# Products of zeros in row tiles of 128, 64 and 32 rows behind the warm-up of an attention and gated-MLP kernel

## The chip, the cores and the metric

The kernel runs on one core of a Trainium2 chip. The metric is the device time of one execution in microseconds (us); lower is better. The core's engines work side by side, each through its own instructions in order: PE (TensorE, matrix products; its loads of weights are listed as PEld), DVE (VectorE), ACT (ScalarE), POOL (GpSimd) and SP (SyncE, which here only issues DMAs). The time before is the median of two runs, 1200.67 us (1200.6 and 1200.75).

## The reference

The inputs are x (2048 tokens of 448 features), wqkv (448 x 1344), wo (448 x 448), W_gate and W_up (448 x 1792), W_down (1792 x 448) and a vector gate_w (448), all float32. An attention block with 16 heads of 28 and a gated MLP are both computed on x and mixed, token by token, by a sigmoid:

```python
x = A_x
g = sigmoid((x * gate_w).sum(-1, keepdims=True))
qkv = (x @ wqkv)                      # split into q, k, v, 16 heads of 28
p = softmax(q @ k.T * 28 ** -0.5)
a = (p @ v) @ wo
gate = x @ W_gate
b = ((gate * (gate > 0)) * (x @ W_up)) @ W_down
return g * a + (1 - g) * b
```

## The kernel before

PE multiplies at its fast rate in the format float32r. To keep float32's accuracy, x, the weights and q and k are split into a high part (the value rounded to float32r, written by ACT in `act_high`, L121) and a low part (the rest, a subtraction on DVE in `low`, L127), and a product of two such numbers is a sum of several products; the table TERMS (L74) lists eleven of them for the 448-deep sums, two chunks of rows being packed together where 64 rows are left over.

The order of all engines' work is written out by hand (`manual_schedule`): an engine executes its instructions in the order in which the kernel's code issues them, and semaphores only make an instruction wait for its operands.

The stages on PE are:

1. A warm-up of WARM = 11 products of a bfloat16 tile of zeros, `warm`, into one PSUM tile (L469 to L472). They need nothing but a memset on DVE, and run while the first loads of x and wq are under way.
2. The projection (`qk`, L427, and `vproj`, L445): for each of four blocks of 512 tokens, seven columns of q and k and the v columns, eleven products each, in PSUM tiles of 512 columns. Each q and k result is copied out by ACT and DVE and sent to DRAM by POOL's queue (L435), and read back by SP's queue as K (L167) and Q (L175). Its last part is mixed with the products that find the scores' maxima (`smax`, L200).
3. The attention, 32 rounds: scores (`score`, L306), their maxima, exponentials on ACT, and P times V (`pv`, L653). In P·V, four products of 32 columns of V each write their own 32 partitions of one PSUM tile; V and P are plain float32 there. The gate and up products of the MLP (L600) fill gaps.
4. The output projection (L852) and the down projection (L893).

The steps around the change, in the order of the code: the loads of the first weights and of x (`load_w`, L341; `load_x`, L377; `load_first`, L459), the warm-up, `make_identity` on POOL, memsets on POOL of rows 96 to 127 of two K tiles and two Q tiles (L479, L480: `f32(K[k])[96:128]` and `f32(QS[k])[96:128]`, k = 0, 1) and of parts of V (L482, L483), the split of the first weights and the first block of x (`split_first`), the split of the second weight chunk (`split_w`), then the first real product group, `qk(0, 0, BY_CHUNK)`, then `split_x(1, x1)`, `load_x(2)` and so on. QS holds the Q tiles, `[128, 4, 512]` in float32r; the second, QS[1], is first filled with a head's q late in the projection.

PSUM has eight banks of 512 float32 columns for each partition. Tiles with the tag "mx" are pairs of banks, of which there are two; they first serve the scores' maxima in the second half of the projection. The warm-up and the first product groups use banks with other tags ("x" and "s").

Of the kernel before, what the change touches and what calls it, by code (L numbers as in the profile page):

```python
# [8 lines left out]
F32 = mybir.dt.float32  # L9
# [9 lines left out]
P = 128  # L19
# [9 lines left out]
TB = 512  # L29
# [55 lines left out]
def gated_mix_kernel(ctx, tc, x, wq, wo, wgu, wd, out):  # L85
    nc = tc.nc
# [3 lines left out]
    psum = ctx.enter_context(tc.tile_pool(name="psum", bufs=1, space=PSUM))  # L90
# [3 lines left out]
    def f32(ap):  # L94
        return ap.bitcast(F32)
# [53 lines left out]
    QS = [vp.tile([P, 4, TB], F32R, name=f"Q{r}") for r in range(2)]  # L149
# [184 lines left out]
    with tc.tile_pool(name="qkv", bufs=1) as pa:  # L334
# [133 lines left out]
        warm = pa.tile([P, TB], BF16, name="warm")  # L468
        nc.vector.memset(warm, 0.0)  # L469
        ps = ps_x("warm_ps")  # L470
        for n in range(WARM):
            nc.tensor.matmul(ps, warm[:, :P], warm, start=True, stop=True)  # L472

        ident = const.tile([P, P], F32, name="ident")
        make_identity(nc, ident)
# [264 lines left out]
    for v, order in enumerate(ROUNDS):  # L740
# [4 lines left out]
        for o in order:  # L745
# [12 lines left out]
            elif o == "x":  # L758
                i, half, n = passes.pop(0)
# [228 lines left out]
```

## Time and profile before

| | |
|---|---|
| median of the runs | 1200.67 us |
| profiled execution: its span, first to last instruction | 1198.9 us |
| granted clock of PE, mean | 1.000 |
| PE products (L600, gate and up) | 1232, busy 364.6 us |
| PE products (L306, scores) | 1024, busy 316.8 us |
| PE products (L653, P·V) | 2048, busy 363.6 us in two groups |
| PE products (L427, q and k) | 308, busy 77.4 us |
| idle time of PE before its first product | 1.2 us, ended by the memset of `warm` |

Every line of a timeline of the profile gives the start in us from the first instruction, the length, the engine, the line of the kernel, the operation, what it writes and reads, "rows*columns" of the weights for PE, the shape of the other operand, how many instructions are merged in the line, and in brackets the idle time of the engine before them and what ended it. The durations of PE's products are modelled ends of a pipeline, so the distance from one start to the next tells more than the length of one. A line of the chain gives start, length and the work that the end of the program hung on at that time. A line of the windows view gives a stretch, its length, the busy time and number of instructions of PE, PEld, DVE, ACT and POOL, PE's granted clock, and the share and rate of the DMA engines.

### The profile page before, as it was taken

How to read it: one execution, taken by the hardware profiler on the slowest of the kernel's cores; microseconds unless marked ns; L12 is line 12 of the kernel's file. 1: busy time of each engine (PE TensorE's matmuls, PEld its weight loads, DVE VectorE, ACT ScalarE, POOL GpSimd, SP SyncE). 2: the span in 40 equal slices, each digit the busy share in tenths (PEclk: the TensorE clock that was granted, in tenths of full speed). 3: DMA queues.
4: the chain of work that ended last, by engine and by line, in shares of the span. 5: the costliest groups of instructions: out<-in, count | busy, mean ns of one | idle time of the engine just before them, and what ended most of it. 6: DMA issues, size and time to landing. Idle time of an engine off the chain costs nothing.

```text
span 1198.9 us, 16948 instructions
## 1 busy us (share of the span) xinstructions
PE 1183.7 (99%) x6183; PEld 820.1 (68%) x6183; DVE 902.8 (75%) x1179; ACT 878.2 (73%) x1082; POOL 748.9 (62%) x326
## 2 busy tenths in 40 slices
PE   9999999999999999999999999999999999999998
PEld 6888755556656666666666666666666666899997
DVE  6466798888898989898888989898988653544242
ACT  5321789999999888888788888888888896422121
POOL 4222387889897777766676767777767786522020
PEclk9999999999999999999999999999999999999999
DMA  9956354354535453443536443436443425743342
GB/s 317 319 207 250 136 191 137 111 141 143 156 129 159 148 163 114 124 122 117 150 119 186 118 129 110 128 117 191 112 126 105 138 89 161 218 136 119 114 128 75
DMA packets 63486, 178.35 MB, mean 149 GB/s; under 512 B 13050, under 2 KB 19650, under 8 KB 58754
## 3 DMA queue, kind: packets, MB, share of 16 engines
q1 hardware_dynamic: 56812, 151.53, 41.1%
q0 software_dynamic: 6160, 25.30, 5.5%
q8 instruction: 48, 0.79, 0.3%
q10 hardware_dynamic: 432, 0.46, 0.1%
q14 instruction: 34, 0.28, 0.1%
HBM read 118.58 MB, written 58.87 MB: 148 GB/s over the span
## 4 chain that ended last, share of the span: by engine, by line
PE 85%; DVE 5%; ACT 3%; DMA 3%; issue 1%; POOL 1%; SPq 1%; DVEq 0%; POOLq 0%; ACTq 0%
PE gu L600 19%; PE s L306 18%; PE po L653 18%; PE sm L200 10%; PE acc L893 10%; PE qk L427 6%; PE wo L852 3%; PE v L445 3%; DVE r L256 1%; ACT P L310 1%; DVE mx L204 1%; ACT P L312 1%; ACT P L296 1%; DMA ls<-os 1%; DMA wor<-wo_d 1%
## 5 line engine op out<-in xcount | busy, mean ns | idle before, releaser
L285 POOL TENSOR_TENSOR P<-P,rm 128x2048 f32<-128x2048 f32 x102 | 470.7, 4633 | 95.5 <-DVE rm L279 79.7
L600 PE MATMUL gu<-X,wg 128*128 128x512 f32 x1232 | 364.6, 395 | 0.7 <-ACT rl L610 0.7
L204 DVE TENSOR_REDUCE mx<-sm 128x1 f32<-128x1024 f32 x256 | 301.5, 1215 | 40.9 <-PE sm L200 40.5
L306 PE MATMUL s<-Q,K 128*128 128x512 f32 x1024 | 316.8, 405 | 6.2 <-ACT V L310 1.9
L600 PEld LDWEIGHTS gu<-X,wg 128*128 128x128 f32 x1232 | 231.2, 188 | 56.7 <-ACT rl L610 2.0
L306 PEld LDWEIGHTS s<-Q,K 128*128 128x128 f32 x1024 | 178.1, 188 | 98.5 <-DVE mn L265 13.4
L312 ACT ACTIVATE P<-s 128x1024 f32<-128x1024 f32 x204 | 202.9, 1031 | 44.2 <-PE s L306 41.6
L653 PE MATMUL po<-P,V 128*32 128x512 f32 x1640 | 227.7, 594 | 0.4 <-ACT P L296 0.4
L296 ACT ACTIVATE P<-P 128x1024 f32<-128x1024 f32 x204 | 213.2, 1072 | 2.1 <-POOL P L285 1.8
L310 ACT ACTIVATE P<-s 128x1024 f32<-128x1024 f32 x206 | 201.5, 1039 | 9.0 <-PE s L306 7.7
L256 DVE SCALAR_TENSOR_TENSOR r<-s,r 128x1024 f32<-128x1024 f32 x124 | 151.6, 1223 | 19.0 <-ACT P L312 10.5
L200 PE MATMUL sm<-K,Q 128*128 128x512 f32 x520 | 163.7, 399 | 0.7 <-DVE mx L204 0.6
L653 PEld LDWEIGHTS po<-P,V 128*32 128x32 f32 x1640 | 63.5, 110 | 116.3 <-issue 108.8
L653 PE MATMUL po<-V 128*32 128x512 f32 x408 | 135.9, 594 | 0.0
L285 POOL TENSOR_TENSOR V<-V,rm 128x2048 f32<-128x2048 f32 x24 | 111.1, 4634 | 23.0 <-DVE rm L279 19.3
L121 ACT ACTIVATE hh<-hr 128x512 fp32r<-128x512 f32 x52 | 32.8, 631 | 117.9 <-PE acc L893 111.8
L200 PEld LDWEIGHTS sm<-K,Q 128*128 128x128 f32 x520 | 91.3, 188 | 33.2 <-ACT P L310 5.6
L127 DVE TENSOR_TENSOR hh<-hr,hh 128x512 fp32r<-128x512 f32 x52 | 47.8, 926 | 82.6 <-ACT hh L121 78.9
L893 PE MATMUL acc<-WD,hh 128*128 128x448 f32 x480 | 100.7, 368 | 0.0
L893 PEld LDWEIGHTS acc<-WD,hh 128*128 128x128 f32 x480 | 90.1, 188 | 8.8
L256 DVE SCALAR_TENSOR_TENSOR r<-s,P 128x1024 f32<-128x1024 f32 x50 | 61.1, 1223 | 38.3 <-ACT P L312 38.3
L271 DVE TRANSPOSE_TENSOR_REDUCE mn<-r 128x32 f32<-128x1024 f32 x63 | 78.0, 1238 | 1.3
(87 smaller groups left out, 1142.6 us busy)
## 6 DMA issues: line engine op xcount, KB each, us to landing
wg<-ws_d SPq DMA_DIRECT2D x42, 896.0 KB
K<-qk_d SPq DMA_DIRECT2D x32, 448.0 KB
Q<-qk_d SPq DMA_DIRECT2D x64, 224.0 KB
h_d<-h SPq DMA_DIRECT2D x56, 256.0 KB
hr<-h_d SPq DMA_DIRECT2D x52, 256.0 KB
ws_d<-wg SPq DMA_DIRECT2D x14, 896.0 KB
qk_d<-st POOLq DMA_DIRECT2D x21, 512.0 KB, 3.2
wgr<-wgu SPq DMA_DIRECT2D x13, 512.0 KB
```

The lines of the kernel that those rows point to most:

```text
L200: nc.tensor.matmul(ps[:, c, :], Q[h][:, u * P:(u + 1) * P], K[h % 3][:, k0:k0 + TB], start=True, stop=True)
L204: nc.vector.tensor_reduce(to, ps, axis=AX.XY, op=OP.max)
L256: nc.vector.scalar_tensor_tensor(r, ps, -1.0, before, op0=OP.mult, op1=OP.min)
L271: nc.vector.tensor_reduce(MN[:, 1:3], R2.pop((v, j)).rearrange("p a (b r) -> p a b r", r=32), axis=AX.X, op=OP.min, apply_transpose=True)
L285: nc.gpsimd.tensor_tensor(QUAD[q], QUAD[q], m, op=OP.subtract)
L296: nc.scalar.activation(q, q, AF.Exp, scale=-SCALE)
L306: nc.tensor.matmul(ps[:, c], K[h % 3][:, k * P:(k + 1) * P], Q[h][:, j * TB:(j + 1) * TB], start=True, stop=True)
L310: nc.scalar.activation(dst, ps, AF.Exp, scale=SCALE)
L312: nc.scalar.activation(dst, ps, AF.Copy, scale=-1.0)
L600: nc.tensor.matmul(ps, WS[i][:, s, a], xf(i // NF, b), start=(n == 0), stop=(n == NT - 1))
L653: nc.tensor.matmul(po[32 * j:32 * j + 32], V[:, h // 4 % 2, k, h % 4], AT.pop((v, k, j)), start=(k == k0), stop=(k == k0 + NK // 2 - 1))
L893: nc.tensor.matmul(ACC[i // NF][t][:, :D], HH[i][:, a, t * P:(t + 1) * P], wd_high_low(f, b), start=(f == 0 and n == 0), stop=(f == NF - 1 ...
```

## The change

Behind the eleven products of the warm-up, 121 more products are issued on PE. For 115 of them both operands are `z`, 512 columns of the second Q tile in float32r, set to zero by one more memset on DVE; they write four banks of the two "mx" tiles, and nobody reads the results. A "place" is one full product of 128 rows, or the two products of 64 rows or four of 32 rows that share those rows: each of them takes its rows of z and has a bank of its own. The list of (rows, count, columns of the weights) has 63 places. Six more products of the bfloat16 zeros follow. Since z lies in QS[1], the memset on POOL at L480 for k = 1, which stands behind it in the code and writes rows 96 to 127 of it, comes after the products on z.

```diff
         for n in range(WARM):
             nc.tensor.matmul(ps, warm[:, :P], warm, start=True, stop=True)
+
+        z = QS[1][:, 0]
+        nc.vector.memset(f32(z), 0.0)
+        four = [psum.tile([P, 2, TB], F32, tag="mx", bufs=2, name=f"four_{k}") for k in range(2)]
+        four = [t[:, k] for t in four for k in range(2)]
+
+        def tiles(rows, count, columns=P):
+            for n in range(count):
+                for k in range(P // rows):
+                    r = slice(k * rows, (k + 1) * rows)
+                    nc.tensor.matmul(four[k if rows < P else n % 4][:columns], z[r, :columns], z[r], start=True, stop=True)
+
+        for rows, count, columns in ((128, 10, 128), (64, 10, 128), (32, 10, 128), (128, 3, 128), (32, 3, 128), (128, 2, 128),
+                                     (32, 1, 128), (128, 2, 128), (128, 10, 64), (128, 10, 32), (128, 2, 128)):
+            tiles(rows, count, columns)
+        for n in range(6):
+            nc.tensor.matmul(four[n % 4], warm[:, :P], warm, start=True, stop=True)
 
         ident = const.tile([P, P], F32, name="ident")
```

## The prediction

> **What bounds the kernel now.** I read the page first (busy shares, then the chain that ended last), then the chain of the first 30 us in order of time, then the PE and PEld timelines around the warm-up. The page:
>
> ```profile
> span 1198.9 us, 16948 instructions
> PE 1183.7 (99%) x6183; PEld 820.1 (68%) x6183; DVE 902.8 (75%) x1179; ACT 878.2 (73%) x1082; POOL 748.9 (62%) x326
> PE 85%; DVE 5%; ACT 3%; DMA 3%; issue 1%; POOL 1%; SPq 1%; DVEq 0%; POOLq 0%; ACTq 0%
> ```
>
> PE is busy 99% of the span and carries 85% of the chain, so work put on PE ahead of everything else is paid unless PE stood idle there. The chain of the first 30 us, with a later row of it for the pace, and PE busy by stage (PE busy and count first in each windows row):
>
> ```profile
> 3.12 5.80 DMA wr<-wq
> ...
> 8.95 0.49 ACT W L121
> ...
> 9.46 0.94 DVE W L127 x2
> 10.40 0.04 issue
> 10.45 19.67 PE qk L427 x84
> ...
> 50.22 2.53 PE qk L427 x11
> ```
>
> ```profile
> 10.40:38.40 28.00, 27.95 (x121) 22.78 (x122) 18.45 (x27) 14.81 (x25) 7.84 (x12) 1.00 0.92 321
> 38.40:120.00 81.60, 81.60 (x374) 69.70 (x373) 48.04 (x51) 18.20 (x47) 17.91 (x27) 1.00 0.68 255
> ```
>
> Until 10.45 us a load of the weights wq and its splitting carry the chain; from 10.45 on the projection's products do, one after another, and PE has no hole up to 120 us. A dense product of 512 columns costs 2.53 / 11 = 0.230 us. What PE does before that:
>
> ```profile
> 0.87 0.27 DVE L469 MEMSET warm<- 128x256 uint32 x1 [0.87 <-PEq L981]
> 1.20 4.10 PE L472 MATMUL warm_ps<-warm 128*128 128x512 bf16 x11 [1.20 <-DVE warm L469]
> 3.74 0.15 PEld L472 LDWEIGHTS <-warm 128*128 128x128 bf16 x1 [0.28 <-issue]
> 4.16 0.15 PEld L472 LDWEIGHTS <-warm 128*128 128x128 bf16 x1 [0.27 <-issue]
> 4.82 0.39 DVE L127 TENSOR_TENSOR W<-wr,W 128x224 fp32r<-128x224 f32 x1 [3.68 <-ACT W L121]
> 5.36 3.53 PE L427 MATMUL qk<-X,W 128*128 128x512 f32 x10
> 9.06 0.49 PE L427 MATMUL qk<-X,W 128*128 128x512 f32 x1 [0.16 <-DVE X L127]
> 9.86 28.57 PE L427 MATMUL qk<-X,W 128*128 128x512 f32 x121 [0.31 <-ACT W L121]
> ```
>
> ```profile
> 4.70 0.38 PE L472 MATMUL warm_ps<-warm 128*128 128x512 bf16 x1
> ...
> 4.92 0.38 PE L472 MATMUL warm_ps<-warm 128*128 128x512 bf16 x1
> ```
>
> The warm-up starts at 0.42 us from product to product (3.74, 4.16) and ends at 0.22 (4.70, 4.92): PE is at its fast pace before the new code begins, and free at 4.92 + 0.22 = 5.14. The first real product starts at 5.36, so PE's hole there is 0.2 us. From then to 10.45 it runs only 10 + 1 + 1 = 12 products, each as its split arrives.
>
> **The change, part by part.**
>
> *Memset of z* (DVE, 128x512 f32): twice the elements of the 0.27 us memset of warm, directly behind it, so about 0.5 us and done by 1.7. DVE's next work starts at 4.82, and PE reaches z at 5.14. Cost 0, hidden by the warm-up; were that cover gone, at most 0.5 us.
>
> *The 63 places.* The list gives 10+10+10+3+3+2+1+2+10+10+2 = 63 places: 19 of full products, 10 of two products of 64 rows, 14 of four products of 32 rows, 20 with 64 or 32 columns of weights. In products these are 19 + 20 + 56 + 20 = 115, all streaming 512 columns in the format of the real products. No row of the trace has fewer than 128 rows. The nearest are those of the P·V products, four column tiles of 32 side by side:
>
> ```profile
> 180.07 7.00 PE po L653 x64
> ```
>
> ```profile
> 180.45 0.13 PEld L653 LDWEIGHTS po<-P,V 128*32 128x32 f32 x4 [0.30 <-issue]
> 180.88 0.13 PEld L653 LDWEIGHTS po<-P,V 128*32 128x32 f32 x4 [0.30 <-issue]
> ```
>
> Four weight loads start together and the next four 0.43 us later, and 64 products take 7.00 us, 0.44 per four: tiles do run at once here. In the code these P and V tiles are plain F32, whereas z, like the operands of the 0.230 us products, is F32R; so I read the 0.43 as the price of the type, not of the tiles. I take a place at one dense product, 0.230 us: 63 x 0.230 = 14.5 us. Ends: 0.22 per place (13.9), and every product for itself, 115 x 0.230 = 26.5.
>
> In a sentence apart: the Trainium skill, TensorE: Matmul & The Clock Gate, Part 3 (Measured speedup vs the span model), gives four row tiles of 32 rows a speed-up of 3.07 rather than 4; by that a place of 32 rows would cost 4 / 3.07 x 0.230 = 0.30, 14 places 1.0 us more, and the sum would be 1216.7; no run here shows it yet.
>
> *Going from one tile size to another.* The sequence has ten such places, seven of rows, three of columns. The P·V stage shows the price:
>
> ```profile
> 179.67 0.40 PE L200 MATMUL sm<-K,Q 128*128 128x512 f32 x1
> 180.00 1.07 PE L653 MATMUL po<-P,V 128*32 128x512 f32 x8
> ...
> 186.47 0.60 PE L653 MATMUL po<-P,V 128*32 128x512 f32 x2
> 187.00 0.73 PE L306 MATMUL s<-Q,K 128*128 128x512 f32 x2
> 187.57 0.62 PE L200 MATMUL sm<-K,Q 128*128 128x512 f32 x2
> ```
>
> Into the narrow tiles: 0.33 from start to start where 0.23 is the pace, 0.10 more. Out of them: 0.53 where 0.43 is the pace, and the first two products take 0.73, not 0.62, as the second weight load was not hidden: together 0.21. The row tiles load 128 columns of weights, so I take 0.2 for each of the seven, 0.1 each for going to 64 and to 32 columns, and 0.2 back: 1.8 us. Ends: 0, and 10 x 0.3 = 3.0.
>
> *Six more warm-up products*: 6 x 0.22 = 1.3 us.
>
> New work on PE: 14.5 + 1.8 + 1.3 = 17.6 us, from 5.14 to 22.7.
>
> *What the delay gives back.* Before, 12 products took 10.45 - 5.14 = 5.31 us because each waited for a split. At 22.7 all of these splits have long been made (the last, of W for the second column block, ends at 9.46 + 1.42 = 10.9, row below), so they take 12 x 0.230 = 2.76. Back: 2.55 us. The last of these waits is what is late in before; behind it nothing is late until X of the second token block:
>
> ```profile
> 9.46 1.42 DVE L127 TENSOR_TENSOR W<-wr,W 128x336 fp32r<-128x336 f32 x4 [0.46 <-ACT W L121]
> 10.08 0.58 ACT L121 ACTIVATE st<-qk 128x512 fp32r<-128x512 f32 x1
> 10.56 2.00 ACT L121 ACTIVATE X<-xr 128x1024 fp32r<-128x1024 f32 x2
> 10.91 0.69 DVE L127 TENSOR_TENSOR st<-qk,st 128x512 fp32r<-128x512 f32 x1
> 11.64 2.36 DVE L127 TENSOR_TENSOR X<-xr,X 128x1024 fp32r<-128x1024 f32 x2
> ...
> 18.20 1.06 ACT L121 ACTIVATE X<-xr 128x1024 fp32r<-128x1024 f32 x1 [3.59 <-DMA xr<-x]
> ```
>
> ACT and DVE take work in order, so this split stands behind the copy of the first product group, which moves with PE. That group ended at 9.06 + 0.49 = 9.55, and the low half of X was whole at 11.64 + 2.36 = 14.0, 4.45 us later (some 4.0 if ACT is free at once, as it is in after). The group that needs it starts one group, 2.53 us, after that end, and reads the second half of the low part from its tenth product, at 2.53 + 9 x 0.23 = 4.6: room of 0.15 to 0.6 us. SP's loads of x and wq wait for the same releases or are already there; POOL's and SP's later issues move along. Cost 0, at most 0.5.
>
> *POOL.* z lies in the second Q tile, so the memset of its rows 96 to 127 now waits for the last product on z:
>
> ```profile
> 6.61 1.81 POOL L480 MEMSET Q<- 32x2048 f32 x1
> 8.48 0.32 POOL L482 MEMSET V<- 128x256 f32 x1
> ...
> 10.30 0.21 POOL L483 MEMSET V<- 128x64 f32 x1
> ...
> 11.91 0.80 POOL L435 DMA_DIRECT2D qk_d<-st  x1 [1.41 <-DVE st L127]
> ```
>
> Behind it on POOL stand eight memsets of V and the first send of q and k. From 22.7 - 1.3 = 21.4 POOL needs 1.81 + (10.51 - 8.48) = 3.8 us, to 25.2; the data of the first send are there at 25.2 + 2.05 (as 11.60 against 9.55 before), 2 us later. Cost 0; without that room the first sends would start later by what is missing.
>
> **Sum.** 17.6 - 2.55 = 15.05 us against the profiled execution: span 1198.9 + 15.05 = 1213.95. Its span is 1.8 us below the median of the two runs, 1200.67; the same 1.8 gives 1215.7 us, 1.3% slower. The rest of the program is fed by these products, so the delay goes through to the end.
>
> **The rivals.**
>
> 1. *The row tiles run one after another* (the other side: slower by more than 2%). The place is the 24 places of 64 and 32 rows. Price: 10 x 1 + 14 x 3 = 52 more products of 0.230, 12.0 us: 1227.7, or 1225.9 if then nothing is drained at a change of size. About 2% is what a measurement of this kernel can tell from no change; that is 1224.7, so the rival decides from 9.0 us on, 0.17 for each of the 52. For it: no row has F32R in tiles, and no row a tile of fewer rows. Against it: the four column tiles above that start together. Chance 0.16.
>
> 2. *Four tiles of 32 rows cost what four column tiles cost*, 0.43: because four weight loads of 128 columns, or eight instructions, are not handed over faster than P·V shows. Price 14 x 0.2 = 2.8: 1218.5. If the 64-row places cost it as well, 2.0 more, 1220.5; if the 20 places with few columns do, 4.0 more, 1224.5. For it: it is the only pace of tiles that the trace shows. Against: the type, as said. Chance 0.22.
>
> 3. *The clock falls during the narrow places.* The last long stretch before the end is 20 places with 64 or 32 columns, 4.6 us; if these count as idle, products go to 0.43 for about as long as the warm-up needed (from 1.20 to between 4.16 and 4.70, 3.2 us, here). Price: up to 3.2 us of half speed in the stretch and again after it, 1.6 + 1.6 = 3.2: 1218.9. Against it: the P·V stage, also in narrow tiles, runs at a granted clock of 1.00 (all four of its column tiles are filled, though). The Trainium skill, TensorE: Matmul & The Clock Gate, Part 1, has the clock follow how busy the array was in the last 3.4 us; the step from 0.42 to 0.22 in the warm-up agrees in its length, and what the monitor makes of a product with few columns no row here shows. Chance 0.04.
>
> 4. *The delay is made good later*, or the places overlap further. For it: the chain has 15% that isn't PE. Against it: from 10.4 to 120 us PE has a hole of 0.05 us in all, and what it waits for later is fed by PE. If a third is made good: 1210.7. Chance 0.06; that it ends over 2% faster 0.01.
>
> **How the numbers follow.** The forecast has 0.52 (own range 1213.5 to 1217.5), rivals 1 to 4 have 0.16, 0.22, 0.04 and 0.06 with 0.01 more for anything faster. Slower by over 2%: rival 1 and a small part of 2, 0.18; faster 0.01; within 2% the rest, 0.81. From 1212.5 to 1227.0 lie the forecast, rivals 2 and 3 and the lower half of 1, some 0.85.
>
> **What would show it.** The first real weight load at about 22.7 us; PE without holes from there; in the places of 32 rows four weight loads within 0.03 us and the next four 0.23 later (0.43: rival 2; one by one at 0.23: rival 1); about 0.1 more to the first product behind each change of size, and 0.1 more to the second; a granted clock of 1.00 up to the first real product; the qk products dense from the first, 12 in 2.8 us; POOL's second Q memset at about 21.4. The prediction is wrong if the qk stage then has holes (a split of X too late), or if the end moves by less than the first real product group.

## The result, and the profile after

| | before | with the change |
|---|---|---|
| median of the first runs | 1200.67 us (2 runs) | 1213.4 us (1211.44 and 1215.37) |
| profiled execution, span | 1198.9 us | 1209.6 us |
| ratio of the times | | 1.0109, 95% interval 1.0068 to 1.015 |

The kernel became 1.1% slower; 1215.7 us was forecast, with a range of 1212.5 to 1227.0. The page of the changed kernel: span, busy shares and the chain by engine.

```profile
span 1209.6 us, 17193 instructions
PE 1195.9 (99%) x6304; PEld 830.9 (69%) x6304; DVE 903.4 (75%) x1180; ACT 878.5 (73%) x1082; POOL 749.5 (62%) x326
PE 89%; DVE 4%; ACT 4%; issue 1%; DMA 1%; POOL 0%; SPq 0%; DVEq 0%; ACTq 0%; POOLq 0%
```

PE is busy 12.2 us more, and the chain now runs through PE from the start. The PE timeline of the changed kernel up to the first real products (lines of the change are L483 and L489 there):

```profile
1.20 3.92 PE L472 MATMUL warm_ps<-warm 128*128 128x512 bf16 x11 [1.20 <-DVE warm L469]
4.77 16.31 PE L483 MATMUL four<-Q 128*128 128x512 f32 x115
20.92 1.47 PE L489 MATMUL four<-warm 128*128 128x512 bf16 x6
22.04 8.22 PE L427 MATMUL qk<-X,W 128*128 128x512 f32 x34
```

The first real product starts at 22.04 us (22.7 forecast), and from there PE has no hole. The weight loads of the new places, in order; in the brackets PEld's idle time before each group:

```profile
4.74 2.26 PEld L483 LDWEIGHTS four<-Q 128*128 128x128 f32 x10
7.36 2.15 PEld L483 LDWEIGHTS four<-Q 64*128 64x128 f32 x20 [0.36 <-issue]
9.87 2.15 PEld L483 LDWEIGHTS four<-Q 32*128 32x128 f32 x40 [0.37 <-issue]
12.37 0.53 PEld L483 LDWEIGHTS four<-Q 128*128 128x128 f32 x3 [0.35 <-issue]
13.27 0.53 PEld L483 LDWEIGHTS four<-Q 32*128 32x128 f32 x12 [0.37 <-issue]
14.16 0.30 PEld L483 LDWEIGHTS four<-Q 128*128 128x128 f32 x2 [0.37 <-issue]
14.82 0.19 PEld L483 LDWEIGHTS four<-Q 32*128 32x128 f32 x4 [0.36 <-issue]
15.26 5.37 PEld L483 LDWEIGHTS four<-Q 128*128 128x128 f32 x24 [0.25 <-issue]
20.91 0.98 PEld L489 LDWEIGHTS <-warm 128*128 128x128 bf16 x6 [0.28 <-issue]
```

Ten places take nearly the same 2.15 to 2.26 us whether they are 10 loads of 128 rows, 20 of 64 or 40 of 32. Each of the seven changes of row size has an idle stretch of 0.25 to 0.37 in front. The last group holds 2 full places, 10 with 64 columns, 10 with 32 and 2 full again: 24 loads without a break, so going to fewer columns is no change of tile size here. Single places of 32 rows, each row from a window of its own:

```profile
10.21 0.19 PEld L483 LDWEIGHTS four<-Q 32*128 32x128 f32 x4
...
10.45 0.19 PEld L483 LDWEIGHTS four<-Q 32*128 32x128 f32 x4
...
10.68 0.19 PEld L483 LDWEIGHTS four<-Q 32*128 32x128 f32 x4
```

Four loads start together and the next four 0.23 later: the row tiles stream side by side at full pace. What stands behind the new work on ACT, DVE and POOL:

```profile
21.14 1.80 POOL L497 MEMSET Q<- 32x2048 f32 x1 [14.47 <-PE four L483]
...
24.83 0.22 POOL L500 MEMSET V<- 128x64 f32 x1
24.98 0.60 ACT L121 ACTIVATE st<-qk 128x512 fp32r<-128x512 f32 x1 [14.91 <-PE qk L427]
25.47 2.00 ACT L121 ACTIVATE X<-xr 128x1024 fp32r<-128x1024 f32 x2
25.61 0.69 DVE L127 TENSOR_TENSOR st<-qk,st 128x512 fp32r<-128x512 f32 x1 [14.84 <-ACT st L121]
26.55 2.36 DVE L127 TENSOR_TENSOR X<-xr,X 128x1024 fp32r<-128x1024 f32 x2 [0.25 <-ACT X L121]
26.61 0.80 POOL L435 DMA_DIRECT2D qk_d<-st  x1 [1.56 <-DVE st L127]
```

POOL's memset waits 14.5 us for the products on z, yet POOL is idle again for 1.56 us before the first send: the cover held.

**Where the end came from.** The starts of the same products in both traces can be set side by side. The thirteenth product of the projection, the first of the dense stretch, starts 14.56 us later; product 5300, at 1012.7 us of before, 14.3 us later; the last one only 10.7 us later. The 3.6 us went in the last stage, behind the one long wait of PE there. That wait, before and then after (PE timelines):

```profile
1046.42 0.68 PE L852 MATMUL wo<-WO,on 128*128 128x448 f32 x2 [1.76 <-POOL on L130]
```

```profile
1059.98 0.67 PE L869 MATMUL wo<-WO,on 128*128 128x448 f32 x2 [0.99 <-POOL on L130]
```

and the pace behind it, the same 168 products in the chains of before, of the change, and of the kernel before profiled once more (below):

```profile
1116.74 34.72 PE acc L893 x168
```

```profile
1128.95 34.04 PE acc L910 x168
```

```profile
1115.55 34.05 PE acc L893 x168
```

34.72 / 168 is 0.2067 us a product, 34.04 / 168 is 0.2026. Over the 719 products behind the wait that is 2.9 us, and the wait itself was 0.8 shorter: together 3.7. The third line shows that the unchanged kernel has the faster pace too, and the changed kernel, profiled again below, has the slower one and a longer wait. So these 3.6 us can't be put down to the change; the 14.3 to 14.6 us that came before them can.

### The profile page after: what moved, and what is told of

The parts are those of the page before. It is cut to its first block, busy times and chain, and to the rows that moved or that the text cites. A ratio compares the mean times of both kernels' runs of the same rounds, so it can differ in the third digit from the quotient of the medians.

```text
span 1209.6 us, 17193 instructions
## 1 busy us (share of the span) xinstructions
PE 1195.9 (99%) x6304; PEld 830.9 (69%) x6304; DVE 903.4 (75%) x1180; ACT 878.5 (73%) x1082; POOL 749.5 (62%) x326
## 4 chain that ended last, share of the span: by engine, by line
PE 89%; DVE 4%; ACT 4%; issue 1%; DMA 1%; POOL 0%; SPq 0%; DVEq 0%; ACTq 0%; POOLq 0%
PE gu L617 21%; PE po L670 18%; PE s L306 18%; PE sm L200 10%; PE acc L910 9%; PE qk L427 6%; PE wo L869 3%; PE v L445 3%; PE four L483 1%; ACT P L310 1%; DVE r L256 1%; DVE mx L204 1%; ACT P L296 1%; ACT P L312 1%; DMA or<-o_d 1%
## 5 line engine op out<-in xcount | busy, mean ns | idle before, releaser
L256 DVE SCALAR_TENSOR_TENSOR r<-s,r 128x1024 f32<-128x1024 f32 x124 | 151.6, 1223 | 18.4 <-ACT P L312 10.7
```

Of the source, the lines that this page charges most:

```text
L256: nc.vector.scalar_tensor_tensor(r, ps, -1.0, before, op0=OP.mult, op1=OP.min)
```

## The experiments

All starts and paces below are from one profile of each kernel. "First real product" is the start of the first q and k product; it was 5.36 us before and 22.04 with the change. PE is free for the new work 0.216 us after the start of the last warm-up product; that was at 4.96 with the change, and is later where the warm-up reached its fast pace later.

**The change again, timed in five rounds** (no edit).

> The changed kernel again. In its first profile PE's dense projection stands 14.5 us later than before, but the last product only 10.7 us later: the products of the last stage run at 0.2027 us each where before has 0.2067 from its wait of 1.8 us for the output projection's operand on. Theory P: this pace is picked anew in each execution when PE restarts behind that wait, and has nothing to do with the change; then the times of several runs fall into two groups, near 1211.5 and near 1215.4 us (and those of before near 1197 and 1200.7), and nothing in between is favoured. Theory Q: the change itself sets the faster pace; then nearly all runs are near 1211.5 and before stays near 1200.7. By both the first real product starts at 22.0 us.

Six runs: 1211.2, 1211.63, 1212.0, 1216.07, 1218.47 and 1218.48 us; the kernel before in eleven runs on the same chip: 1197.43 to 1201.81, median 1199.39. Ratio 1.0119, interval 1.0097 to 1.0141. The six runs lie in three groups rather than two, and before reaches down to 1197.4: Q falls. P is borne out only in part, as the eleven runs of before lie in no groups at all. The first real product started at 22.34, 0.3 later than expected, because the warm-up got to its fast pace later (PE was free at 5.26 instead of 4.96). The profile was taken of one of the two longest runs (span 1216.7); it shows what made that one long, in PE's waits and in the windows around them (granted clock third from the end of a row):

```profile
PE wo L869 <- POOL on L130: 3.1, 1, 3.1
```

```profile
1062.80:1066.10 3.30, 3.30 (x10) 2.92 (x11) 0.33 (x1) 0.00 (x0) 2.42 (x2) 0.50 0.59 165
1066.20:1100.00 33.80, 33.80 (x165) 30.71 (x164) 14.23 (x19) 7.59 (x11) 7.37 (x6) 1.00 0.39 119
```

Here the wait was 3.1 us, and then the clock was granted at 0.50 for 3.4 us. With the slow pace behind it, the last product stands 17.7 us later than before, although its dense projection stood 14.9 later.

**The kernel before again** (no edit).

> The kernel before, profiled once more. P: its last stage runs at 0.2027 or at 0.2067 us a product, span 1195 to 1196 or 1199. Q: 0.2067 and 1199. By both PE's dense projection starts at 10.4 to 10.5 us.

Its dense projection starts at 10.28 us, a little before the 10.4 expected; its late pace is 0.2027 (the third chain line above) and its span 1196.3. This is one of the two outcomes that P allows, and not Q's.

**All products of a place on one row group.**

```diff
-                    r = slice(k * rows, (k + 1) * rows)
+                    r = slice(0, rows)
```

> The same products, but all two or four of a place take rows 0 to 63, or 0 to 31, so they share one row group; the banks stay four. Theory: products overlap because they use different row groups; here they go one after another, 52 more by 0.230 us = 12.0, and the first real product starts at 34.0 us instead of 22.0. Rival: it is the narrower row tile itself (or the bank of its own) that lets the next product in early; then it stays at 22.0.

The first real product started at 47.06 us. The products do go one after another, 0.227 from start to start in the stretches at full clock, which excludes the rival; but the 34.0 of the theory was far too little, because the clock fell (windows, granted clock third from the end):

```profile
8.10:12.70 4.60, 4.60 (x21) 3.61 (x20) 2.54 (x7) 1.39 (x5) 0.00 (x0) 1.00 0.88 318
12.90:15.80 2.90, 2.90 (x14) 2.35 (x14) 0.00 (x0) 0.00 (x0) 0.00 (x0) 1.00 0.00 0
15.80:27.70 11.90, 11.90 (x29) 8.67 (x27) 0.00 (x0) 0.00 (x0) 0.00 (x0) 0.50 0.01 1
```

The first row is the twenty products of 64 rows, the others those of 32. From 15.8 to 43.1 us the clock was 0.50 and products went by at 0.427: 27.3 x (1 - 0.230 / 0.427) = 12.6 us lost. With 12.0 for the products and 0.7 because the warm-up got fast later, that makes 25.3 of the 25.0 measured.

**z in plain F32.**

```diff
-        z = QS[1][:, 0]
-        nc.vector.memset(f32(z), 0.0)
+        z = f32(QS[1][:, 0])
+        nc.vector.memset(z, 0.0)
```

> z taken as plain F32 instead of F32R, all else as in the change. Theory: 0.43 us, as in P times V, is the price of the type; then all 63 places cost 0.43, about 27.1 us, with ten changes of tile size by 0.2 = 2.0 and 1.3 for the last six, and the first real product starts at 35.3 us. Rival: 0.43 is the price of column tiles; full and row places stay at 0.23, the 20 places of few columns cost 0.43, and the first real product starts at 26.0 to 26.6 us.

The first real product started at 63.18 us; both numbers were wrong. The weight loads of some places of 32 rows, and of some with 64 and 32 columns:

```profile
24.10 0.20 PEld L483 LDWEIGHTS four<-Q 32*128 32x128 f32 x4 [0.22 <-issue]
24.53 0.20 PEld L483 LDWEIGHTS four<-Q 32*128 32x128 f32 x4 [0.22 <-issue]
```

```profile
50.17 0.14 PEld L483 LDWEIGHTS four<-Q 128*64 128x64 f32 x1 [0.29 <-issue]
50.60 0.14 PEld L483 LDWEIGHTS four<-Q 128*64 128x64 f32 x1 [0.29 <-issue]
51.55 0.14 PEld L483 LDWEIGHTS four<-Q 128*32 128x32 f32 x2 [0.81 <-issue]
52.01 0.11 PEld L483 LDWEIGHTS four<-Q 128*32 128x32 f32 x1 [0.32 <-issue]
```

Every step costs 0.43, in row tiles, with few columns, and (not shown) with full rows: the price is the type's, as the prediction read it, and not that of tiles. What the expectation missed is that a plain F32 product is issued as two instructions (230 for the 115 products), so a place costs 0.86: 63 x 0.86 = 54 us, of the 57.3 from the first of them at 5.86 to 63.18. In this type, few columns are a tile size of their own: 0.81 of idle before the first load of 32 columns, where the F32R kernel has none.

**Ten full places alone.**

```diff
-        for rows, count, columns in ((128, 10, 128), (64, 10, 128), ...
-            tiles(rows, count, columns)
-        for n in range(6):
-            nc.tensor.matmul(four[n % 4], warm[:, :P], warm, start=True, stop=True)
+        tiles(128, 10)
```

> Of the new work only ten places of full products; no row tiles, no few columns, no last six. Theory: what stands before the first real product is free as long as its first twelve products still wait for splits; ten places are 2.3 us, PE is free at about 7.3, and the dense projection starts at 10.4 to 10.6 us as before, so the cost is 0 to 0.2 us. Rival: each product put on PE ahead is paid in full; then the dense projection starts at 12.7 us.

The weight loads of the first real products:

```profile
4.82 2.24 PEld L483 LDWEIGHTS four<-Q 128*128 128x128 f32 x10
7.10 2.77 PEld L427 LDWEIGHTS qk<-X,W 128*128 128x128 f32 x12
10.27 1.70 PEld L427 LDWEIGHTS qk<-X,W 128*128 128x128 f32 x8 [0.40 <-DVE W L127]
```

The ten cost nothing: the real products start 2.0 us later, at 7.32, run twelve in a row, wait for the same split of W, and the dense stretch begins at 10.27, where the kernel before has 10.45 and, profiled again, 10.28. The rival's 12.7 falls. (Its whole time, 1200.66 us in one run, says nothing of this: its granted clock was 0.50 for 3.4 us behind the late wait.)

**A change of tile size at every place.**

```diff
-        for rows, count, columns in ((128, 10, 128), (64, 10, 128), ...
-            tiles(rows, count, columns)
+        for n in range(31):
+            tiles(128, 1)
+            tiles(32, 1)
+        tiles(128, 1)
```

> 63 places again, but one full place and one of four tiles of 32 rows in turn, 62 changes of tile size instead of seven. Theory: a change costs what it shows in the changed kernel's profile, 0.33 us from a full product to the first tile and 0.43 to 0.44 from a tile place of one to the next full product, 0.76 a pair; 31 pairs are 23.6 us and the first real product starts at 30 to 31 us. Rival: the price is paid once for a run of many, because the queue behind it has to be refilled; single places then go by at 0.23 and the first real product starts at 21 to 22 us.

The first real product started at 33.52 us. Some places out of the middle:

```profile
28.16 0.19 PEld L483 LDWEIGHTS four<-Q 32*128 32x128 f32 x4 [0.25 <-issue]
28.59 0.19 PEld L483 LDWEIGHTS four<-Q 128*128 128x128 f32 x1 [0.24 <-issue]
29.03 0.19 PEld L483 LDWEIGHTS four<-Q 32*128 32x128 f32 x4 [0.25 <-issue]
```

0.43 a place either way, 0.87 a pair, not 0.76: the expectation left out that a place's weight load, too, stays unhidden after each change. So a change costs 0.20 wherever it stands, and the rival (a price for long runs only) falls. 62 x 0.20 + 63 x 0.23 + 1.3 are 28.2 us; counted from PE's release, here at 5.31, that leads to 33.5.

**Long narrow stretches.**

```diff
-        for rows, count, columns in ((128, 10, 128), (64, 10, 128), ...
+        for rows, count, columns in ((128, 1, 128), (32, 30, 128), (128, 2, 128), (128, 30, 32)):
```

> 63 places again: one full, 30 of four tiles of 32 rows, two full, 30 with 32 columns of weights, then the last six. Each narrow stretch lasts 6.9 us, longer than the 3.4 us for which the clock stayed halved in another run, whereas in the change the stretch of 32 rows lasts 2.5 us and that of few columns 4.6. In the run where all products share one row group the granted clock fell to 0.5 about 2.9 us into the products of 32 rows. Theory: four row tiles side by side, and full rows with few columns, count as busy; the clock stays at 1.0, and with two changes of tile size the first real product starts at 21.0 to 21.5 us (plus up to 0.6 for the phase of the warm-up). Rival (the prediction's third): a stretch of narrow tiles counts as idle; the clock falls to 0.5 in one of them, its places go to 0.43, and the first real product starts at 24 us or later.

```profile
5.40:12.20 6.80, 6.80 (x111) 5.71 (x113) 4.95 (x11) 3.73 (x10) 1.26 (x1) 1.00 0.98 351
12.90:19.80 6.90, 6.90 (x33) 3.34 (x30) 0.00 (x0) 0.00 (x0) 0.00 (x0) 1.00 0.00 1
```

The clock stays at 1.00 in 6.8 us of four row tiles and in 6.9 us of 32 columns; the first real product starts at 21.63 us, 0.66 of it because the warm-up got fast later (PE free at 5.61 instead of 4.96), about what was allowed for that. The rival falls.

**The output projection later, without and with the change.**

```diff
-    for tb, load, split, at in ((0, 4, (7, 8), (10, 11, 12, 13)), ...
+    for tb, load, split, at in ((0, 4, (7, 8), (12, 12, 13, 13)), ...
```

> The kernel before, with the first token block's output projection two steps later in the down projection (steps 12, 12, 13, 13 instead of 10, 11, 12, 13), so that PE has other products while its operand on is made. Theory P: the wait of 1.4 to 3.5 us goes, PE doesn't restart, its pace stays at 0.2027 us a product to the end, and all runs lie within 1 us near 1196 us. Theory Q (the pace is drawn independently of that wait): runs still differ by some 3 us, 1196 to 1199.5. Third: the products moved up wait for something else, and 1198 to 1200 us is left.

> The change with the same later output projection. P: 14.5 to 14.8 us above the kernel without the zeros and with the same move, with a spread of the runs under 1 us, near 1210.7 us. Q: the runs spread by 3 to 7 us as those of the change do.

Without the zeros: 1195.86 to 1199.67 us in twelve runs, median 1197.42, against 1198.57 for the kernel before in 17 runs (1197.48 to 1203.09); ratio 0.9986, interval 0.9974 to 0.9998. With the zeros: 1211.33, 1211.33, 1211.63 and 1212.61. In both profiles the long wait is gone (the longest hole there is 0.44 and 0.89 from start to start), the late pace is 0.2027, and the spans are 1194.4 and 1209.6, 15.2 us apart, as their dense projections are 15.3 apart. The medians with and without the zeros are 14.06 us apart. The gain from taking the wait away, 1.15 us of the median, is small, and its interval nearly reaches 1. P's "within 1 us" failed: twelve runs still spread by 3.8 us, 1195.9 to 1199.7, which is what theory Q said. The four runs with the zeros spread by 1.3 us, more than P's 1 and less than Q's 3. What the longer runs did was not seen, as the profile fell on a short one. A small hole can be enough: in the profile of the long narrow stretches the pace went to 0.2067 behind a hole of 0.43 from start to start, at 1159 us, and back to 0.2027 behind the next, of 0.42. Whether the longer runs here did the same stays open.

## Why the prediction was right

*Bound.* PE carries the start, and delay there goes through: the shift at the thirteenth product and at product 5300 was 14.56 and 14.33 us in the change, 26.05 and 25.50 with a change of tile size at every place, 39.59 and 39.57 on one row group. Rival 4 (made good later) is out up to the last stage; what moved there also moves without the change.

*The 63 places.* 0.230 each was taken against ends of 0.22 and one product after another. The last warm-up product, the last product of zeros and the thirteenth real product in the changed kernel's profile:

```profile
4.74 0.38 PE L472 MATMUL warm_ps<-warm 128*128 128x512 bf16 x1
...
22.01 0.38 PE L489 MATMUL four<-warm 128*128 128x512 bf16 x1
...
25.01 0.62 PE L427 MATMUL qk<-X,W 128*128 128x512 f32 x2
```

At 0.216 from start to start, PE is free for the zeros at 4.96 and for the real products at 22.22. (The record of the first real product stands at 22.04, only 0.03 behind the last product of zeros, so PE can't have been free for it yet.) The new work took 17.27 us; without 1.31 for the last six and seven changes at 0.20 there remain some 14.6, 0.231 a place. The forecast had 14.5. The reading of P·V's 0.43 as a price of the type was the choice that mattered, though 0.43 turned out to be one of the two instructions of a plain F32 product; rival 2, which took it for one of tiles, would have added 2.8 or more. The Trainium skill's 3.07 for four row tiles (TensorE: Matmul & The Clock Gate, Part 3) isn't borne out in a running stream: four products of 32 rows per 0.23 us are a factor of 4.

*Changes of size.* 1.8 us were forecast, of which seven of rows at 0.2 were right and the 0.4 for columns too much: 0.

*What the delay gives back.* 2.55 us forecast; 17.27 - 14.56 = 2.71 measured. The twelve products took 25.01 - 22.22 = 2.79 (2.76 forecast), and the room was 0.18 larger because PE was free at 4.96, not 5.14. Ten places alone, shorter than that, were free.

*Covers.* The split of X was whole at 26.55 + 2.36 = 28.9 us and PE had no hole; POOL had 1.56 us to spare where 2 were forecast.

*Sum.* 15.05 us forecast for the dense projection, 14.56 measured. Of the difference, 0.3 is work that was sized too large (0.4 for the columns, the places a little too little), and 0.18 the earlier release. That release was luck: in the two other profiles with the same zeros, the change again and the one with the later output projection, it came at 5.26 and 5.59, and the dense projection stood 14.9 and 15.2 later than before. In all three it starts 20.05 to 20.06 after the release (2.76 + 17.6 = 20.36 forecast). The medians of the five rounds, 1214.04 and 1199.39, are 14.65 apart, but the first of them lies between two groups of runs.

*The end, and luck.* The prediction named as a sign against itself an end that moves by less than the first real product group. In the first pair of profiles this sign appeared: the last product moved by 10.7, the dense projection by 14.56. It is not the size of the change, because the profiled run of before had the slow late pace and that of the change the fast one and a shorter wait; in the second profile of the change the last product moved by 17.7. The prediction knew nothing of two paces. Of its two first runs with the change one, 1211.44, lies below the stated range and only their median inside it, and the base of 1200.67 is 1.3 to 2.1 us above the later medians of the same kernel. The work ahead of the projection was forecast rightly; that the two medians were 12.7 apart and not further off is partly luck.

*Rival 1* was ruled out, but its price was mis-sized: on one row group the products of 64 and 32 rows cost some 24 us more, not 12, since those of 32 rows also halve the clock. *Rival 3* named the right mechanism for the wrong products: products of 32 rows one at a time halve the clock, row tiles side by side and few columns don't. (The chances as stated add up to 1.01.)

## What to carry to other kernels

Work ahead of the first real product is free as far as the products behind it still wait for their operands, and is paid one to one from there on; the room is the time from PE's release to its dense stretch, less what those products take when nothing holds them. Row tiles of 64 or 32 rows in float32r, each with its own row group, cost one full product for all of them, and 0.2 us each time the tile size changes: keep tiles of a size together. (Each had a bank of its own here too; whether they need it was not tested.) Where an end time moves by another amount than the place of the change shows, follow the same product through both traces before giving the rest a cause, and time the unchanged kernel more than twice.

## What the runs showed of the hardware

- Two paces of one and the same dense stream: 0.2067 and 0.2027 us for a product of 448 columns, at a granted clock of 1.00, each often kept for hundreds of products. In the last stage of all eleven profiles the pace changes only behind a hole in PE's work (0.2 us and more), and it differs between executions of the same kernel. What chooses it was not settled.
- The granted clock fell to 0.50 within 2.9 us of products of 32 rows, one at a time, though PE was never idle; twenty products of 64 rows (4.6 us) before them did not lower it, nor did four of 32 rows side by side or full rows with 32 columns. It also fell, for 3.4 us, behind a wait of PE of 3.1 us and behind two of 2.0 and 2.1, and did not behind another of 2.0 nor behind shorter ones. The Trainium skill (TensorE: Matmul & The Clock Gate, Part 1) has the activity judged in windows of 3413 ns that run by themselves; the 3.4 us, and a wait of 2.0 that falls on either side, agree.
- Plain F32 takes two instructions of 0.43 us a product against one of 0.23 in float32r; and a weight tile of 64 or 32 columns is a tile size of its own in plain F32 but not in float32r.
